# Half F tile of w3 for two chunks at once, a reordered start, and a last output in two pieces (linear attention block with MLP, one Trainium2 core)

## The chip, the cores and the metric

The kernel runs on one core of a Trainium2 chip. The metric is device microseconds of one execution; the numbers quoted are medians or means of several executions, and where two kernels are compared they were run in turn on the same chip.

TensorE (PE in the profile) is the engine everything turns on here; VectorE is DVE, ScalarE is ACT, GpSimd is POOL, and SyncE (SP) issues most of the DMA transfers.

## The reference, cut to what matters

`x` is 2048 tokens by 640, in bf16. One branch is linear attention (32 heads of 20) and ends in a product with `wo`; the other is a normalised, shifted two-layer MLP and then a second MLP through a width of 1728. A gate mixes the two.

```python
def _A_ref(x, wqkv, wo):                        # q, k, v = x @ wqkv
    phi = lambda t: jnp.where(t > 0, t + 1, jnp.exp(t)) + 1e-6
    ...
def _B_ref(x, w1, w2, w3, w4):
    ...
    x1 = x + hs                                 # hs: shifted gelu(LN(x) @ w1) @ w2
    h2 = _gelu(_layernorm(x1) @ w3) @ w4        # w3: 640 x 1728, w4: 1728 x 640
    return x1 + h2
g = sigmoid((x * gate_w).sum(-1, keepdims=True))
return g * _A_ref(x, wqkv, wo) + (1 - g) * _B_ref(x, w1, w2, w3, w4)
```

1728 is 13 tiles of 128 and a half tile of 64.

## The kernel before: the parts that matter

A scheduler in Python places work items (a group of matmuls and its evictions) in one order per engine. All matmul groups share a helper, so in the profile most of them have one line, L606. Tokens are handled in 16 tiles (`NT`) of 128 and 4 chunks (`NCH`) of 512; `KD` is 5 slices of the 640 columns; `KFF` is 13.

The start. Two loads of x rows come first, then the five slices of the query weights. While they are in flight TensorE multiplies constants ("fillers", `warmup`), so that it is busy when the work arrives. The four x tiles of the first chunk are transposed on TensorE (`t_x`, copied out by DVE for even tiles and ACT for odd ones). A small DMA ("touch") reads a few scattered pieces of the weights.

```python
    sch.dma("act", junk[:, 0, 0:32].rearrange("p (k f) -> p k f", k=2),
            A_wqkv.rearrange("(k p) f -> p k f", p=128)[:, 0:KD:KD - 1, 0:16], "touch")
    dma_in(x_tok[:, 0:2, :], x2[0:256, :]..., "x01")
    dma_in(x_tok[:, 2:4, :], x2[256:512, :]..., "x23")
    for k in range(KD):
        load_wq(k)
    # ... (key weights, gate vector)
    for c in range(1, NCH):
        dma_in(x_tok[:, 4 * c:4 * c + 4, :], x2[512 * c:512 * (c + 1), :]..., "xc%d" % c)
        for t in range(4 * c, 4 * c + 4):
            sch.dma("sp", xT[:, :, 128 * t:128 * (t + 1)], x_tok[:, t, :], ..., transpose=True)
    # ... (cut)
    NWARM = 5
    NWARM2 = 2
    # ... (cut)
    addA(("warm",), 0.0, lambda: warmup(NWARM, 427.0))
    for i in range(4):
        addA(("tx", i), 0.28, lambda i=i: t_x(i))
        if i % 2:
            addA(("warm", i), 0.0, lambda: warmup(NWARM2, 300.0))
    addA(("q", 3), 5.44, q_four)     # queries of the tiles 0 to 3, slice by slice
    addA(("k", 0), 1.36, k_first)
    for i in range(1, 4):
        addA(("k", i), 1.36, lambda t=i: k_tile(t))
```

The half tile. A matmul here has 64 weight columns and writes 64 of the 128 output partitions (`ps[64 * par:64 * par + 64]`), so two matmuls of 256 columns are placed side by side, one on each half, once per chunk. In the chain before, ten of them take 0.67 us; one after the other, at half the 0.216 us of a 512-column matmul each, they would need 1.08 us (estimate):

```python
    def w3_half(c):
        b = bank()
        jobs = []
        for k in range(KD):
            xv = xnT[:, k, 512 * c:512 * (c + 1)].rearrange("p (n h q) -> p n h q", h=2, q=128)
            for par in range(2):
                jobs.append((ps[64 * par:64 * par + 64, b, 0:256], w3[:, k, 128 * KFF:F], xv[:, :, par, :],
                             k == 0, k == KD - 1))
        # ... (ten matmuls, one per job)
        activation(h2h[:, sl, :], ps[:, b, 0:256], ACTF.Gelu_apprx_tanh)
```

The end. The last tile is evicted in two pieces (512 and 128 columns), then stored by one DMA:

```python
    def out_tiles(t0, t1):
        sch.dma("sp", out[0, 128 * t0:128 * t1, :]..., x_tok[:, t0:t1, :], ...)
```

## Time and profile before

| | before |
|---|---|
| time, median of 3 | 266.43 us (265.92 to 266.44) |
| profiled execution | 266.35 us, span 264.6 us, granted clock 1.0 |
| TensorE busy | 260.2 us, 98% |
| chain of waits | 98% TensorE |
| half tile | 4 excursions of 0.67 us |
| last eviction starts | 261.12 us |

The profile page of the kernel before. The digits are the busy share in 40 slices, in tenths; the chain is the work that ended last, followed backwards.

```profile
span 264.6 us, 4340 instructions
...
PE 260.2 (98%) x1729; PEld 136.7 (52%) x1729; DVE 145.8 (55%) x242; ACT 107.9 (41%) x218; POOL 91.4 (35%) x148
...
PE   7999999999999999999999999999999999999995
...
PEclk9999999999999999999999999999999999999999
...
PE 98%; DVE 0%; POOL 0%; issue 0%; POOLq 0%
```

TensorE is at 90% or more in every slice between the first and the last. Time can only be won by taking TensorE work away, before the first useful matmul, or after the last one. PEclk is the clock that the profile reports as granted: full speed everywhere.

The chain of waits of the kernel before; columns are start (us), duration (us), and what it was.

```profile
3.91 1.25 PE ps L617 x10
5.15 0.73 PE ps L833 x2
5.88 0.56 PE ps L617 x10
6.44 0.43 PE ps L833 x2
...
13.68 6.83 PE ps L606 x50
...
134.52 0.67 PE ps L1024 x10
...
169.85 0.67 PE ps L1024 x10
...
205.18 0.67 PE ps L1024 x10
...
240.51 0.67 PE ps L1024 x10
...
261.12 1.08 DVE x_tok L645 x2
```

The first lines are the start: ten transposes (L617), two fillers (L833), ten transposes, two fillers, after five fillers that are not shown; the queries follow. "L606 x50" at 13.68 is the first stage of dense keys; I use its first line as the moment when the start is over. L1024 are the four half tiles. The eviction of the last tile is the final line. From 13.68 to 261.12 us are 247.44 us. What follows the start of that eviction is 266.35 - 261.12 = 5.23 us of the time.

The timeline of TensorE in the kernel before: start, time until the group ends, what.

```profile
3.91 1.25 PE L617 MATMUL ps<-ident,x_tok 128*128 128x128 bf16 x10
...
5.72 0.72 PE L617 MATMUL ps<-ident,x_tok 128*128 128x128 bf16 x10
...
6.71 0.38 PE L855 MATMUL ps<-wq,xT 128*128 128x512 bf16 x1
6.92 0.22 PE L856 MATMUL ps<-wq,xT 128*128 128x128 bf16 x1
6.98 0.38 PE L855 MATMUL ps<-wq,xT 128*128 128x512 bf16 x1
```

The queries start at 6.71 us, and the next instructions follow 0.21 and 0.06 us later (such a time from one matmul's start to the next is its pitch), 0.216 and 0.056 us over the stage.

The DMA issues in the last stretch of the kernel before: size of one and microseconds from issue to landing.

```profile
out_dram<-x_tok SPq DMA_DIRECT2D x2, 160.0 KB, 1.8
```

The last of these two stores is what the end of the execution waits for: 1.8 us, of which its data move for 0.55 us (263.0 to 263.55).

### The profile page before, as it was taken

How to read it: one execution, taken by the hardware profiler on the slowest of the kernel's cores; microseconds unless marked ns; L12 is line 12 of the kernel's file. 1: busy time of each engine (PE TensorE's matmuls, PEld its weight loads, DVE VectorE, ACT ScalarE, POOL GpSimd, SP SyncE). 2: the span in 40 equal slices, each digit the busy share in tenths (PEclk: the TensorE clock that was granted, in tenths of full speed). 3: DMA queues.
4: the chain of work that ended last, by engine and by line, in shares of the span. 5: the costliest groups of instructions: out<-in, count | busy, mean ns of one | idle time of the engine just before them, and what ended most of it. 6: DMA issues, size and time to landing. Idle time of an engine off the chain costs nothing.

```text
span 264.6 us, 4340 instructions
## 1 busy us (share of the span) xinstructions
PE 260.2 (98%) x1729; PEld 136.7 (52%) x1729; DVE 145.8 (55%) x242; ACT 107.9 (41%) x218; POOL 91.4 (35%) x148
## 2 busy tenths in 40 slices
PE   7999999999999999999999999999999999999995
PEld 4555555555555555554445445545454455445553
DVE  1486877899713797999776986321212121122242
ACT  3496677741365757766651211212321322121000
POOL 4003995759764025688730204000120011021020
PEclk9999999999999999999999999999999999999999
DMA  7765998634567897255456831120000200002011
GB/s 229 218 100 133 199 182 136 191 85 22 102 122 106 252 379 137 39 99 49 92 113 126 111 63 25 42 85 2 0 0 11 90 0 0 2 0 102 0 50 50
DMA packets 50627, 24.78 MB, mean 94 GB/s; under 512 B 42028, under 2 KB 49197, under 8 KB 50608
## 3 DMA queue, kind: packets, MB, share of 16 engines
q1 hardware_dynamic: 49184, 21.23, 37.0%
q0 software_dynamic: 1152, 3.28, 5.4%
q8 instruction: 13, 0.21, 0.4%
q14 instruction: 6, 0.05, 0.1%
q10 hardware_dynamic: 272, 0.01, 0.1%
HBM read 12.05 MB, written 2.62 MB: 55 GB/s over the span
## 4 chain that ended last, share of the span: by engine, by line
PE 98%; DVE 0%; POOL 0%; issue 0%; POOLq 0%
PE ps L606 61%; PE ps L1102 21%; PE ps L785 8%; PE ps L855 2%; PE ps L833 1%; PE ps L1084 1%; PE ps L1024 1%; PE ps L617 1%; PE ps L941 1%; PE ps L856 1%; DVE x_tok L645 0%; POOL ones_c L665 0%; POOLq L1228 0%
## 5 line engine op out<-in xcount | busy, mean ns | idle before, releaser
L662 ACT ACTIVATE h2T<-ps 128x512 bf16<-128x512 f32 x52 | 31.0, 596 | 83.8 <-PE ps L606 83.7
L606 PE MATMUL ps<-xnT,w_58 128*128 128x512 bf16 x260 | 60.9, 379 | 0.0
L1102 PE MATMUL ps<-w_84,h2T 128*128 128x512 bf16 (+1 forms) x416 | 58.8, 299 | 0.0
L628 POOL TENSOR_SCALAR abx<-x_tok,stg 128x640 f32<-128x640 bf16 x16 | 13.9, 873 | 107.6 <-DVE x_tok L645 71.2
L1102 PEld LDWEIGHTS ps<-w_84,h2T 128*128 128x128 bf16 x416 | 32.7, 98 | 27.8 <-issue 1.3
L645 DVE SCALAR_TENSOR_TENSOR x_tok<-ps,stg,abx 128x640 bf16<-128x640 f32 (+2 forms) x17 | 14.3, 845 | 51.7 <-PE ps L1102 51.7
L606 PEld LDWEIGHTS ps<-xnT,w_58 128*128 128x128 bf16 x260 | 24.0, 98 | 24.8 <-issue 1.0
L645 DVE SCALAR_TENSOR_TENSOR abx<-ps,stg,abx 128x640 f32<-128x640 f32 x16 | 14.1, 882 | 27.9 <-PE ps L606 24.9
L662 ACT ACTIVATE Er<-ps 128x640 bf16<-128x640 f32 x32 | 22.4, 704 | 13.7 <-PE ps L606 8.8
L662 ACT ACTIVATE hsT<-ps 128x512 bf16<-128x512 f32 (+1 forms) x32 | 18.9, 593 | 14.6 <-PE ps L606 14.3
L661 ACT ACTIVATE junk<-x_tok 128x640 bf16<-128x640 bf16 x32 | 23.6, 736 | 2.0 <-DVE x_tok L643 1.7
L606 PE MATMUL ps<-M_sb,pqnT 128*128 128x512 bf16 (+1 forms) x160 | 24.0, 299 | 0.0
L606 PE MATMUL ps<-xnT,w_59 128*128 128x512 bf16 x100 | 23.9, 379 | 0.0
L785 PE MATMUL ps<-pk_tok,x_tok 128*128 128x512 bf16 (+1 forms) x160 | 23.9, 299 | 0.0
L606 PE MATMUL ps<-w_60,hsT 128*128 128x512 bf16 (+1 forms) x160 | 23.7, 299 | 0.0
L606 PE MATMUL ps<-wkg,xT 128*128 128x512 bf16 (+1 forms) x150 | 22.6, 300 | 0.0
L628 POOL TENSOR_SCALAR xn<-x_tok,st_54 128x640 bf16<-128x640 bf16 x16 | 17.3, 1087 | 7.1 <-DMA xnT<-xn 7.0
L606 PEld LDWEIGHTS ps<-w_60,hsT 128*128 128x128 bf16 x160 | 13.2, 98 | 12.2
L606 PEld LDWEIGHTS ps<-M_sb,pqnT 128*128 128x128 bf16 x160 | 13.1, 98 | 12.2 <-issue 0.6
L628 POOL TENSOR_SCALAR xn<-x_tok,st_55 128x640 bf16<-128x640 bf16 x16 | 16.7, 1052 | 5.1 <-DMA xnT<-xn 4.7
L606 PE MATMUL ps<-wq,xT 128*128 128x512 bf16 (+1 forms) x120 | 18.3, 299 | 0.0
L628 DVE TENSOR_SCALAR Er<-Er 128x640 bf16<-128x640 bf16 x32 | 12.0, 376 | 10.2 <-ACT Er L662 10.0
(74 smaller groups left out, 264.5 us busy)
## 6 DMA issues: line engine op xcount, KB each, us to landing
w_58<-in_B_w_dram SPq DMA_DIRECT2D x1, 2160.0 KB, 8.6
w_84<-in_B_w_dram SPq DMA_DIRECT2D x1, 2080.0 KB, 14.2
x_tok<-in_A_x_dram SPq DMA_DIRECT2D x3, 640.0 KB, 5.9
out_dram<-x_tok SPq DMA_DIRECT2D x3, 640.0 KB, 3.5
wq<-in_A_wqkv_dram SPq DMA_DIRECT2D x5, 160.0 KB, 3.8
wkg<-in_A_wqkv_dram SPq DMA_DIRECT2D x5, 160.0 KB, 3.7
wv<-in_A_wqkv_dram POOLq DMA_DIRECT2D x1, 800.0 KB, 6.0
wo_aug<-in_A_wo_dram POOLq DMA_DIRECT2D x5, 150.0 KB, 4.9
```

Source lines behind the costliest of these rows:

```text
L606: ins = e.matmul(out_ap, l, r, start=(i == 0), stop=(i == n - 1))
L617: ins = e.transpose(o, s_, ident[:])
L628: return engf(lambda e: e.tensor_scalar(out_ap, in_ap, s1, s2, op0, op1), rd, [out_ap], cost=cost)
L645: return dve(lambda e: e.scalar_tensor_tensor(out_ap, in0, scalar, in1, op0, op1), rd, [out_ap], cost=cost)
L661: return act(lambda e: e.activation(out_ap, in_ap, func, bias=bias, scale=scale, accum_out=accum), rd, wr, cost=cost)
L662: return act(lambda e: e.activation(out_ap, in_ap, func, bias=bias, scale=scale), rd, wr, cost=cost)
L785: ins = e.matmul(o, l, r, start=(t0 + q_ == 0), stop=(t0 + q_ == NT - 1))
L833: ins = e.matmul(ps[:, b, :], ones_c[:, 0:128], ones_c[:, 128:640], start=True, stop=True)
L855: e.matmul(ps[:, b, 0:512], l, w[:, k, 0:512], start=(k == 0), stop=(k == KD - 1))
L856: return e.matmul(ps[:, b + 1, 0:n2], l, w[:, k, 512:512 + n2], start=(k == 0), stop=(k == KD - 1))
L941: ins = e.matmul(o, l, r_, start=st_, stop=sp_, skip_group_check=True)
L1102: ins = e.matmul(o, l, r, start=False, stop=(i == KFF - 1))
```

## The change

Three independent parts, each meant to save TensorE time or exposed time at an end:

1. `w3_half` works on two chunks (512 columns) at a time: two excursions instead of four, with the same matmul columns in all. The halves of chunk 1 must be ready earlier, so dependencies move.
2. The first slice of the query weights is loaded between the two x pairs; the queries of the tiles 0 and 1 with that slice take the place of the last two fillers. The touch reads 80 pieces instead of 256.
3. The last output is stored in two pieces, the first while the second eviction runs.

```diff
-    h2h = rb.alloc("h2h", [128, 2, 256], BF16)
+    h2h = rb.alloc("h2h", [128, NCH, 256], BF16)
...
-    sch.dma("act", junk[:, 0, 0:32].rearrange("p (k f) -> p k f", k=2),
-            A_wqkv.rearrange("(k p) f -> p k f", p=128)[:, 0:KD:KD - 1, 0:16], "touch")
+    sch.dma("act", junk[0:16, 0, 0:80].rearrange("p (k f) -> p k f", k=KD),
+            A_wqkv[:, 0:16].rearrange("(k e r) f -> e r k f", k=KD, r=8)[:, 0, :, :], "touch")
     dma_in(x_tok[:, 0:2, :], ...)
+    load_wq(0)
     dma_in(x_tok[:, 2:4, :], ...)
-    for k in range(KD):
+    for k in range(1, KD):
         load_wq(k)
...
-    def stream(tiles, w, n2, land, done):          # order made by an assumed landing time
+    def stream(order, w, n2, done):                # order given; (t, None) transposes tile t
...
     def q_four():
-        stream(range(4), wq, 128, 0.5, lambda t, b: phi(b, pq_tok[:, t, :]))
+        order = [(0, 0), (1, 0), (2, None), (3, None), (0, 1), (1, 1), (2, 0), (0, 2), (1, 2), (3, 0), (0, 3), ...]
+        stream(order, wq, 128, lambda t, b: phi(b, pq_tok[:, t, :]))
...
-    for i in range(4):
+    for i in range(2):
         addA(("tx", i), 0.28, lambda i=i: t_x(i))
-        if i % 2:
-            addA(("warm", i), 0.0, lambda: warmup(NWARM2, 300.0))
+    addA(("warm", 1), 0.0, lambda: warmup(NWARM2, 300.0))
...
-            xv = xnT[:, k, 512 * c:512 * (c + 1)].rearrange("p (n h q) -> p n h q", h=2, q=128)
+            xv = xnT[:, k, 512 * c:512 * (c + 2)].rearrange("p (n h q) -> p n h q", h=2, q=128)
...
-                jobs.append((ps[64 * par:64 * par + 64, b, 0:256], ...))
+                jobs.append((ps[64 * par:64 * par + 64, b, :], ...))
...
+        dst = out[0, 128 * t0:128 * t1, :].rearrange("(n p) d -> p n d", p=128)
+        for n0, n1 in ((0, 512), (512, D)) if t0 == NT - 1 else ((0, D),):
+            sch.dma("sp", dst[:, :, n0:n1], x_tok[:, t0:t1, n0:n1], ...)
...
-        IT.add("W3", ("w3h", c), 0.76, lambda c=c: w3_half(c))
+        if c % 2 == 0:
+            IT.add("W3", ("w3h", c), 1.27, lambda c=c: w3_half(c), [(("t2", u), 0.9) for u in range(4 * c + 4, 4 * c + 8)])
...
-        deps4 = [(("a", t), 0.0), (("w3h", c), GEL)]
+        deps4 = [(("a", t), 0.0), (("w3h", c - c % 2), GEL), (("w3", c, KFF - 1), GEL)]
```

More of the change, by code (lines that the diff above doesn't have):

```diff
@@ L842, in q_tile @@
         phi(b, pq_tok[:, t, :])
-    def stream(tiles, w, n2, land, done):
-        nxt = {t: 0 for t in tiles}
-        bs = {t: pair() for t in tiles}
-        now = 0.0
-        while nxt:
-            t = next((t for t in tiles if t in nxt and nxt[t] * land <= now), min(nxt, key=lambda t: nxt[t]))
-            now = max(now, nxt[t] * land) + 0.272
-            k, b = nxt[t], bs[t]
+    def stream(order, w, n2, done):
+        bs = {}
+        for t, k in order:
+            if k is None:
+                t_x(t)
+                continue
+            if k == 0:
+                bs[t] = pair()
+                bank_hold.update((bs[t], bs[t] + 1))
+            b = bs[t]
             l = xT[:, k, 128 * t:128 * (t + 1)]
@@ L857, in stream @@
             pe(fn, [w[:, k, 0:512 + n2], l], [ps[:, b, 0:512], ps[:, b + 1, 0:n2]], cost=272.0)
-            nxt[t] += 1
-            if nxt[t] == KD:
-                del nxt[t]
+            if k == KD - 1:
+                bank_hold.difference_update((b, b + 1))
                 done(t, b)
     def q_four():
-        stream(range(4), wq, 128, 0.5, lambda t, b: phi(b, pq_tok[:, t, :]))
+        order = [(0, 0), (1, 0), (2, None), (3, None), (0, 1), (1, 1), (2, 0), (0, 2), (1, 2), (3, 0), (0, 3), (1, 3), (0, 4),
+                 (2, 1), (1, 4), (2, 2), (2, 3), (2, 4), (3, 1), (3, 2), (3, 3), (3, 4)]
+        stream(order, wq, 128, lambda t, b: phi(b, pq_tok[:, t, :]))
     def k_out(t, b):
@@ L870, in k_first @@
     def k_first():
-        stream(range(1), wkg, 131, 0.0, k_out)
+        stream([(0, k) for k in range(KD)], wkg, 131, k_out)
     def addA(name, dur, fn, deps=()):
@@ L1011, in w3_half @@
     def w3_half(c):
-        sl = c % 2
         b = bank()
@@ L1015, in w3_half @@
         for k in range(KD):
-            xv = xnT[:, k, 512 * c:512 * (c + 1)].rearrange("p (n h q) -> p n h q", h=2, q=128)
+            xv = xnT[:, k, 512 * c:512 * (c + 2)].rearrange("p (n h q) -> p n h q", h=2, q=128)
             for par in range(2):
-                jobs.append((ps[64 * par:64 * par + 64, b, 0:256], w3[:, k, 128 * KFF:F], xv[:, :, par, :],
-                             k == 0, k == KD - 1))
+                jobs.append((ps[64 * par:64 * par + 64, b, :], w3[:, k, 128 * KFF:F], xv[:, :, par, :], k == 0, k == KD - 1))
         def fn(e):
@@ L1025, in fn @@
             return ins
-        pe(fn, [w3[:, :, 128 * KFF:F], xnT[:, :, 512 * c:512 * (c + 1)]], [ps[:, b, 0:256]], cost=KD * 112.0 + 200.0)
-        activation(h2h[:, sl, :], ps[:, b, 0:256], ACTF.Gelu_apprx_tanh)
+        pe(fn, [w3[:, :, 128 * KFF:F], xnT[:, :, 512 * c:512 * (c + 2)]], [ps[:, b, :]], cost=KD * 218.0 + 200.0)
+        activation(h2h[:, c:c + 2, :].rearrange("p c n -> p (c n)"), ps[:, b, :], ACTF.Gelu_apprx_tanh)
     qn_slot = {}
@@ L1078, in w4_half @@
                 rows = slice(64 * par, 64 * par + 64)
-                jobs.append((ps[:, bs[2 * par + i], 0:n1 - n0], h2h[rows, sl, 128 * pr:128 * (pr + 1)], w4[rows, KFF, n0:n1]))
+                jobs.append((ps[:, bs[2 * par + i], 0:n1 - n0], h2h[rows, t // 4, 128 * pr:128 * (pr + 1)], w4[rows, KFF, n0:n1]))
         def fn(e):
@@ L1085, in fn @@
             return ins
-        pe(fn, [h2h[:, sl, 128 * pr:128 * (pr + 1)], w4[:, KFF, :]], [j[0] for j in jobs], cost=490.0)
+        pe(fn, [h2h[:, t // 4, 128 * pr:128 * (pr + 1)], w4[:, KFF, :]], [j[0] for j in jobs], cost=490.0)
     def w4_tile(t):
@@ L1115, in out_tiles @@
     def out_tiles(t0, t1):
-        sch.dma("sp", out[0, 128 * t0:128 * t1, :].rearrange("(n p) d -> p n d", p=128), x_tok[:, t0:t1, :], "out%d" % slot("out", 4))
+        dst = out[0, 128 * t0:128 * t1, :].rearrange("(n p) d -> p n d", p=128)
+        for n0, n1 in ((0, 512), (512, D)) if t0 == NT - 1 else ((0, D),):
+            sch.dma("sp", dst[:, :, n0:n1], x_tok[:, t0:t1, n0:n1], "out%d" % slot("out", 4))
     def w3_load():
```

## The prediction

> **What bounds it.** TensorE. The page gives PE 98% of a 264.6 us span at full clock; the chain of waits is 98% PE. So a gain must remove TensorE time, or lie before the first useful matmul (about 6.7 us) or after the last (about 261.9 us).
>
> **Part 1, half F tile of w3.** Four excursions of ten 128x256 matmuls (64 weight columns, two side by side) become two of ten 128x512. In the chain an excursion takes 0.67 us and the 15 matmuls behind it 2.54 us. A full 512-column matmul has a pitch near 0.216 us (1.08 us for five), a 128-column one near 0.056 us, so those 15 should take 2.44 us: 0.10 us to leave the mode. Five side-by-side pairs of 256 columns need 0.54 us (estimate, half of 1.08), so entering costs 0.13 us. Together about 0.23 us per excursion, two of which go: -0.47 us, all on the critical path. [...] the 0.23 us here is this case's price. The order of instructions moves: attention output tile 1 now precedes the first w4 tile. Its transposed input was issued at 136.4 us and takes 2.7 us; the tile would start near 140.3 us, so about 1 us is spare.
>
> **Part 2, start.** In the timeline before: five filler matmuls from 1.59 us, ten transposes 3.91, two fillers 4.95, ten transposes 5.72, two fillers 6.28, dense queries from 6.71 us. The last two fillers (0.43 us) go: queries of tiles 0 and 1 with slice 0 fill the place, and transposes of tiles 2 and 3 follow. The slice is needed at 5.7 us; issued second (near 1.3 us) with 3 to 3.8 us to landing, it is there by about 4.5 to 5.1. x rows 2-3 slip to about 5.3 us, needed at 6.3. ScalarE's copy of tile 1 ends at 5.89 us, just in time. Gain -0.43 us; the stream behind is dense, so it carries through. The lighter touch (80 small pieces, not 256) may bring the first x rows slightly earlier: 0 to -0.15 us. The gate vector lands near 11.4 us and is needed at 11.7: tight.
>
> **Part 3, end.** The last eviction ends at 262.20 us; the store is issued then, its data move 263.0 to 263.55 us, landing 1.8 us after issue. In two pieces, 512 columns go out from 261.85 us during the second eviction, and only 128 columns remain. The first's issue slot (0.37 us) delays the second by about 0.05 us. [...] Most of the 1.8 us is fixed. -0.1 us (0 to -0.25).
>
> **Sum.** -0.47 - 0.43 - 0.05 - 0.1 = about -1.05 us, from 266.43: **265.4 us**, range 264.9 to 265.95. Faster by over 2%: 0.01; within 2%: 0.98; slower: 0.01.
>
> **What would show it.** Right: two w3-half groups of about 1.2 us in the chain; x20 instead of x40; the dense query stage starting at 5.7 us and key tile 0 at 11.7 us; PE still at 98% with no new waits; last store data ending near 263.3 us minus the shift.
>
> **What would make it wrong.** A PE wait for wq slice 0, x rows 2-3 or an xT copy at 5.7 to 8 us; the gate vector late; the moved attention and w4 tiles waiting for VectorE to free PSUM banks near 150 us, where VectorE runs 3 us chains between evictions; the narrow store taking as long as the wide one.

The sum came to -0.47 - 0.43 - 0.05 - 0.1 = -1.05 us, from 266.43 to 265.4 us. The -0.05 us for the lighter touch and the -0.1 us for the end were guesses. That most of the 1.8 us is fixed rests on the 0.55 us in which the data move.

Only executions in the fast state are compared.

## The result and the profile after

| | before | after |
|---|---|---|
| time, median of 6 fast runs in turn | 266.64 us (265.92 to 266.87) | 266.3 us (266.11 to 266.51) |
| profiled execution | 266.35 us, span 264.6 | 266.33 us, span 264.6 |
| TensorE busy | 260.2 us, 98% | 258.2 us, 98% |
| dense key stage starts | 13.68 us | 14.36 us |
| last eviction starts | 261.12 us | 261.32 us |

The ratio is 0.999, with a 95% interval from 0.9976 to 1.0004. Ratios here are the mean time of one kernel's fast runs over the mean of the other's fast runs of the same rounds, so not quite the ratio of the quoted medians. Executions in which one die ran at a lower clock are left out of the means. The prediction, 265.4 us with a range of 264.9 to 265.95, is missed: 266.3 lies above it. The means differ by 0.27 us, with an interval that includes no gain at all, where 1.05 us had been announced.

The page after:

```profile
span 264.6 us, 4264 instructions
...
PE 258.2 (98%) x1675; PEld 136.4 (52%) x1707; DVE 145.9 (55%) x242; ACT 107.6 (41%) x216; POOL 91.1 (34%) x148
...
PE 96%; DMA 1%; issue 1%; ACT 0%; DVE 0%
```

The matmul count falls by 54, the count of weight loads (PEld) by 22. The 22 are real: 20 half-tile matmuls (20 left of 40) and two fillers. The other 32 are matmul records missing from this trace, so the busy time is not compared closely, and that is also where the bits of "issue" in this chain come from that lower its TensorE share to 96%; another 1% is a DMA, which comes next.

The chain of waits after:

```profile
0.80 3.27 DMA x_tok<-in_A_x_dram
...
4.12 1.25 PE ps L617 x10
...
14.36 3.17 PE ps L606 x22
...
135.20 1.20 PE ps L1025 x10
...
205.62 1.20 PE ps L1025 x10
...
261.32 1.08 DVE x_tok L645 x2
```

Two half-tile groups of 1.20 us replace four of 0.67. From 14.36 to 261.32 us are 246.96 us, against 247.44 before: the middle became 0.48 us shorter. After the start of the last eviction, 266.33 - 261.32 = 5.01 us follow, against 5.23: 0.22 less. And the start became 0.68 us longer, 14.36 against 13.68. Those three make up -0.02 us, which is the whole difference of the two profiled executions. **The gain was made and is in the trace; in this pair the first 14 us took it back.** The chain also begins with a new line: TensorE now waits for the first x rows.

The timeline of TensorE after:

```profile
4.12 1.25 PE L617 MATMUL ps<-ident,x_tok 128*128 128x128 bf16 x10 [0.21 <-DMA x_tok<-in_A_x_dram]
...
6.01 0.63 PE L858 MATMUL ps<-wq,xT 128*128 128x512 bf16 x1
6.44 0.31 PE L859 MATMUL ps<-wq,xT 128*128 128x128 bf16 x1
6.54 0.63 PE L858 MATMUL ps<-wq,xT 128*128 128x512 bf16 x1
...
7.08 1.02 PE L617 MATMUL ps<-ident,x_tok 128*128 128x128 bf16 x10
7.93 0.38 PE L858 MATMUL ps<-wq,xT 128*128 128x512 bf16 x1
8.15 0.22 PE L859 MATMUL ps<-wq,xT 128*128 128x128 bf16 x1
```

The plan worked as a sequence: queries at 6.01 us, before the second ten transposes. But the pace is wrong. The first 512-column matmul has 0.43 us to its successor (6.01 to 6.44), where in the kernel before it had 0.21. The ten transposes at 7.08 take 1.02 us, against 0.72. Only from 7.93 on does a 512-column matmul again take 0.22 us. TensorE ran at half its pace until about 7.7 us.

The granted clock for two stretches of that same profile (time, busy us and count, clock, DMA share, GB/s):

```profile
core 0: us, PE busy (x), PEclk, DMA share, GB/s
1.50:4.30 2.80, 2.50 (x7) 1.00 0.66 220
4.30:7.70 3.40, 3.40 (x22) 1.00 0.99 336
```

The clock column says 1.00 in both, though the matmuls in them came at half pace (0.427 us from one of 512 columns to the next). In this stretch the matmul pitch, not that column, tells the pace. The expectations below call the moment at which the pitch falls the release of the clock. That a clock changes there is not shown, since the column reads 1.00 before the moment and after it.

The DMA issues at the end, after:

```profile
out_dram<-x_tok SPq DMA_DIRECT2D x1, 128.0 KB, 1.7
out_dram<-x_tok SPq DMA_DIRECT2D x1, 32.0 KB, 1.5
```

The store that the end waits for now carries 32 KB and lands in 1.5 us rather than 1.8, with rows of 256 bytes.

### The profile page after: what moved, and what is told of

Its sections match the earlier page's. It is cut to its first block, busy times and chain, and to the rows that moved or that the text cites. A ratio compares the mean times of both kernels' runs of the same rounds, so it can differ in the third digit from the quotient of the medians.

```text
span 264.6 us, 4264 instructions
## 1 busy us (share of the span) xinstructions
PE 258.2 (98%) x1675; PEld 136.4 (52%) x1707; DVE 145.9 (55%) x242; ACT 107.6 (41%) x216; POOL 91.1 (34%) x148
## 4 chain that ended last, share of the span: by engine, by line
PE 96%; DMA 1%; issue 1%; ACT 0%; DVE 0%
PE ps L606 60%; PE ps L1103 21%; PE ps L786 8%; PE ps L858 2%; DMA x_tok<-in_A_x_dram 1%; PE ps L1085 1%; PE ps L1025 1%; PE ps L617 1%; PE ps L859 1%; PE ps L944 1%; DVE x_tok L645 0%; PE ps L834 0%; ACT h2T L662 0%; ACT M_sb L662 0%
## 5 line engine op out<-in xcount | busy, mean ns | idle before, releaser
L606 PE MATMUL ps<-xnT,w_58 128*128 128x512 bf16 x250 | 59.0, 379 | 0.5
L1103 PE MATMUL ps<-w_84,h2T 128*128 128x128 bf16 (+1 forms) x412 | 58.2, 298 | 0.4 <-issue 0.3
L606 PE MATMUL ps<-M_sb,pqnT 128*128 128x128 bf16 (+1 forms) x157 | 23.7, 298 | 0.2
L606 PE MATMUL ps<-w_60,hsT 128*128 128x128 bf16 (+1 forms) x158 | 23.6, 298 | 0.1
L786 PE MATMUL ps<-pk_tok,x_tok 128*128 128x128 bf16 (+1 forms) x156 | 23.3, 297 | 0.2
L606 PE MATMUL ps<-xnT,w_59 128*128 128x512 bf16 x96 | 23.2, 379 | 0.3 <-issue 0.2
L606 PE MATMUL ps<-wkg,xT 128*128 128x131 bf16 (+1 forms) x148 | 22.4, 298 | 0.1
L606 PEld LDWEIGHTS ps<-M_sb,pqnT 128*128 128x128 bf16 x160 | 13.3, 98 | 12.4 <-issue 0.4
L606 PEld LDWEIGHTS ps<-w_60,hsT 128*128 128x128 bf16 x160 | 13.3, 98 | 12.2
L606 PE MATMUL ps<-wq,xT 128*128 128x128 bf16 (+1 forms) x118 | 18.2, 298 | 0.1
```

Source lines behind the costliest of these rows:

```text
L606: ins = e.matmul(out_ap, l, r, start=(i == 0), stop=(i == n - 1))
L786: ins = e.matmul(o, l, r, start=(t0 + q_ == 0), stop=(t0 + q_ == NT - 1))
L1103: ins = e.matmul(o, l, r, start=False, stop=(i == KFF - 1))
```

## The experiments

Two numbers help to read all of them. In the fast profiles the dense middle had the same length to 0.01 us wherever its code was the same and no new wait fell in it: 247.44 us without the halves, 246.96 with them. After the start of the last eviction came 5.22 to 5.27 us without the split store and 4.98 to 5.01 with it (one outlier: 6.17 us in the profiled execution of the light touch, the excess lying outside its span). So for each kernel I subtract the middle and the end (5.22 or 5.00) from its mean time and get the mean **start**, the moment when the dense keys begin, over all its fast runs and not just the profiled one (this takes it that the middle and end are as long in the unprofiled runs; a new wait in the middle of such a run is counted into its start). For before it is 266.45 - 247.44 - 5.22 = 13.79 us (55 runs in five jobs, each on another chip). The prediction amounts to a start of 13.2 to 13.3.

| kernel | mean us | minus before of the same job | implied start |
|---|---|---|---|
| halves alone | 266.50 | +0.01 | 14.32 |
| end alone | 266.21 | -0.27 | 13.77 |
| halves and end | 265.76 | -0.73 | 13.80 |
| halves and end, again | 265.88 | -0.43 | 13.92 |
| halves and end, one more filler | 265.70 | -0.89 | 13.74 |
| start alone | 266.52 | +0.03 | 13.86 |
| start alone, again | 266.50 | +0.06 | 13.84 |
| start alone, one more filler | 266.65 | +0.22 | 13.99 |
| the change, first job | 266.29 | -0.27 | 14.33 |
| the change, again | 265.89 | -0.70 | 13.93 |
| light touch alone | 267.19 | +0.76 | 14.53 |
| new order alone, old touch | 266.49 | +0.05 | 13.83 |
| halves, end, new order, old touch | 265.63 | -0.96 | 13.67 |
| the same again | 265.80 | -0.61 | 13.84 |
| the same, last two x chunks loaded together | 265.81 | -0.60 | 13.85 |
| before, no touch | 266.72 | +0.41 | 14.06 |
| before, one filler instead of five | 267.36 | +0.76 | 14.70 |

The first four have a start whose code is that of before, and yet lie between 13.77 and 14.32. That is the scatter of one kernel's mean over six runs, and nothing smaller than about 0.3 us is read from a single row.

### Each part alone

Theory: halves and end gain what they should, and the start gives nothing or costs. Rival: the halves' new dependencies, or the attention tile that now comes earlier, cost something in the middle.

Halves alone (the `h2h`, `w3_half`, `w4_half` and dependency lines of the change, nothing else):

```diff
-            xv = xnT[:, k, 512 * c:512 * (c + 1)]...
+            xv = xnT[:, k, 512 * c:512 * (c + 2)]...
(and the other lines of part 1)
```

> Before plus the merged w3 halves alone. Theory A (each excursion left out saves 0.23 us) and theory B (the late clock release at the start ate the gain) both say: 0.45 us faster than before. If it is the same as before within 0.1 us, the halves are where the gain was lost. Profile: two w3-half pieces of 1.20 us in the chain. The clock release (pitch of 512-column matmuls falling from 0.43 to 0.22 us) is at about 5.6 us as before if it depends on the program; anywhere between 4 and 8 us if it is chance.

Measured: 266.50 us, ratio 1.0001 (0.998 to 1.0021): nothing in the mean. Its chain shows why:

```profile
5.26 0.85 PE ps L833 x2
6.11 0.80 PE ps L617 x10
...
14.15 6.83 PE ps L606 x50
...
134.99 1.20 PE ps L1022 x10
...
205.41 1.20 PE ps L1022 x10
...
261.11 1.08 DVE x_tok L645 x2
```

From 14.15 to 261.11 us are 246.96 us: the 0.48 us are there. But the start, whose instructions are those of before, took 0.47 us longer in this execution: the ten transposes took 0.80 us at 6.11 against 0.56 at 5.88, and two fillers 0.85 against 0.73; the first transposes also began 0.10 us later (4.01 us). The same code starts at 13.68 in one execution and 14.15 in another. This was the first sight of a chance in the start that the prediction hadn't reckoned with.

Start alone (the touch, the load order, `stream`, `q_four` and the first items):

```diff
+    load_wq(0)
     dma_in(x_tok[:, 2:4, :], ...)
(and the other lines of part 2)
```

> Before plus the new start with the new touch alone. Theory B, the new start delays the release of the clock: 0.3 to 0.7 us slower than before, first k tile by x5 groups from about 14.3 us instead of 13.7, release near 7.7 us as in after. Rival, the late release in the one profile of after was chance: 0.2 to 0.5 us faster than before on average.

Measured: 266.52 us over five fast runs, ratio 1.0 (0.998 to 1.002). One run was slow (275.22 us), and the profile fell on it. Part 2 on its own gains nothing that shows.

End alone (`out_tiles` only):

```diff
+        for n0, n1 in ((0, 512), (512, D)) if t0 == NT - 1 else ((0, D),):
```

> Before plus the last output in two pieces alone. Expected from the pair of profiles (3.48 us from the start of the last eviction to the end of the span before, 3.28 after): 0.1 to 0.2 us faster. Rival, that the fixed completion latency is all: 0.0.

Measured: 266.21 us, -0.27, ratio 0.9989 (0.997 to 1.0008). The mean is not decisive. In the profile the eviction starts at 260.93 us and the execution takes 265.92: 4.99 us, against 5.23. The 0.24 us is well outside the 0.05 us by which that stretch varies. The 32 KB piece landed 1.5 us after issue, against 1.8 for the 160 KB of the tile before, so the latency is mostly, but not wholly, the same for both sizes.

Halves and end:

```diff
(the lines of parts 1 and 3)
```

> After with the start undone (halves and tail only). Theory B: 0.6 us faster than before, 0.3 us faster than after. Rival (chance): 0.6 us faster than before, but 0.2 to 0.4 slower than after on average.

Measured: 265.76 us, -0.73, ratio 0.9972 (0.9948 to 0.9996). The sum of the two readings is -0.48 - 0.23 = -0.71. In this profile too the middle took 246.96 us. The rival, a cost in the middle, falls.

### The start, taken apart

Light touch alone, on before:

```diff
-    sch.dma("act", junk[:, 0, 0:32]..., A_wqkv...[:, 0:KD:KD - 1, 0:16], "touch")
+    sch.dma("act", junk[0:16, 0, 0:80]..., A_wqkv[:, 0:16]...[:, 0, :, :], "touch")
```

> Before with the lighter touch alone (80 pieces on 16 partitions for 256 on 128). So far the first x rows landed at 3.9 to 4.0 us after the span's start in four profiles with the old start and at 4.12 and 4.17 us in two with the new one. Theory T (the touch does it): landing at 4.1 to 4.2 us here, and the time 0.1 to 0.3 us longer than before. Theory O (the order of the loads does it): 3.9 us as before, time the same as before or up to 0.1 us shorter.

Measured: 267.19 us, +0.76, ratio 1.0028 (1.0006 to 1.005). The first transposes started at 4.18 us after a wait of 0.29 us for x, against 3.91 before. Lighter was not earlier. A part of the +0.76 is the scatter described above, and 0.16 us of it is the one run (268.13 us, the profiled one) whose excess lies outside its span.

The new order alone, with the old touch:

```diff
(part 2 without the two touch lines)
```

> The new order of loads and of the first queries with the old touch. Theory T: first x rows at 3.9 us, dense stage up to 0.4 us earlier than before at the same clock release, mean time 0.2 to 0.4 us shorter than before. Theory O: first x rows at 4.1 to 4.2 us, mean time within 0.2 us of before.

Measured: 266.49 us, +0.05, ratio 1.0 (0.998 to 1.002). The profile caught an execution with an early full pace:

```profile
5.41 0.38 PE L858 MATMUL ps<-wq,xT 128*128 128x512 bf16 x1
5.63 0.22 PE L859 MATMUL ps<-wq,xT 128*128 128x128 bf16 x1
5.81 0.39 PE L858 MATMUL ps<-wq,xT 128*128 128x512 bf16 x1
```

The queries begin at 5.41 us and their pitch is 0.22 us at once. Here the start is what the prediction had drawn, and dense keys begin at 12.92 us in the timeline (13.52 before). But 0.13 us passes between 5.63 + 0.06 and 5.81: the query of tile 1 waits for ScalarE's copy of its transposed x. And the gain was lost again at 42 us, where the chain runs through a DMA:

```profile
28.86 8.21 DMA x_tok<-in_A_x_dram
...
37.09 5.31 DMA xT<-x_tok
...
42.44 2.90 PE ps L606 x20
```

The third x chunk was issued at 28.86 us and landed 8.2 us later; the transposes behind it in the queue came late, and the dense keys waited for tile 12 (0.7 us in the view of waits; the stretch from the dense keys to the last eviction is 0.92 us longer than in before). An early TensorE alone doesn't make this wait: in before the same chunk landed in 6.0 us and its transposes began at 35.07 us, 2 us earlier than here.

Start alone again, and with a sixth filler to close the gap ahead of the x rows:

```diff
-    NWARM = 5
+    NWARM = 6          # second kernel only
```

> The whole new start once more (its first profile fell into the slow state). If the release of the clock is chance in both kernels, the mean is 0.2 to 0.4 us shorter than before (0.43 us of fillers less, half to all of 0.2 us of later x rows back). If the new start delays the release, the mean is the same or up to 0.5 us longer and the release lies after 6.5 us.

Measured: 266.50 us, +0.06, ratio 1.0002 (0.9982 to 1.0022). The result of the first try stands, this time with a fast profile: full pace from 5.60 us, first transposes at 4.15 us, after a wait of 0.25 us for x.

> The whole new start with six fillers ahead of the first transposes instead of five, so that the gap of 0.2 to 0.4 us in which PE waits for the first x rows is closed. If a gap in PE's activity delays the release of the clock: mean 0.3 us or more shorter than the new start with five, release at 5.0 to 6.5 us. If the release is a matter of chance alone: within 0.15 us of it.

Measured: 266.65 us, +0.22, ratio 1.0008 (0.9989 to 1.0026). Filling the gap gained nothing that shows. In its profile the first transposes still began at 4.17 us, and the full pace came at 6.14.

### When the full pace comes

From the starts of successive matmuls in each trace I read the moment at which the pitch of a 512-column matmul falls from 0.427 to 0.216 us, called the release below. (Before: 5.63 us; after: 7.71.) At a pitch of 0.427 us the matmuls take twice as long as at 0.216, so a release one microsecond later costs about half a microsecond (estimate from the two pitches, the half rule below). The release, and the start of the dense keys in the timeline:

| profile | first transposes | release | dense keys | dense keys minus half the release |
|---|---|---|---|---|
| old start: before | 3.91 | 5.63 | 13.52 | 10.71 |
| end alone | 3.86 | 5.32 | 13.33 | 10.67 |
| halves and end | 3.89 | 5.15 | 13.27 | 10.70 |
| halves alone | 4.01 | 6.53 | 13.99 | 10.73 |
| halves and end, again | 3.89 | 7.05 | 14.19 | 10.67 |
| old order, light touch | 4.18 | 7.09 | 14.36 | 10.82 |
| new order and light touch: after | 4.12 | 7.71 | 14.20 | 10.35 |
| after, again | 4.15 | 7.09 | 13.91 | 10.37 |
| start alone, again | 4.15 | 5.60 | 13.30 | 10.50 |
| start alone, one more filler | 4.17 | 6.14 | 13.47 | 10.40 |
| new order, old touch | 4.05 | 4.60 | 12.92 | 10.62 |
| halves, end, new order, old touch | 3.86 | 4.92 | 12.97 | 10.51 |
| the same again | 4.01 | 4.72 | 13.07 | 10.71 |
| the same, last two x chunks loaded together | 4.05 | 6.60 | 13.64 | 10.34 |

In the first five rows only the release differs, and the last column stays within 0.06 us while the keys move by 0.9. So the release accounts for the spread of the old start. (Left out are the profiles with another number of fillers on the old start, with no touch, or with earlier x chunks.)

For one and the same release, the rows with the new order lie 0 to 0.36 us below the 10.70 of the old start. The three with the earliest release (4.60 to 4.92 us) gain least, 0 to 0.19: there TensorE waits for ScalarE's copy of the transposed x (0.13, 0.26 and 0.18 us), and in "the same again" 0.1 us more for the x rows of tile 2, which landed at 6.19 us where the prediction had about 5.3. The four with a release after 6 us gain 0.30 to 0.36. A part of what is missing to the predicted 0.43 goes with the light touch: against the one profile with it and the old order (10.82), the four rows with the new order and the light touch lie 0.32 to 0.47 us lower. So beside the same touch and with a late release the order's price comes out about right; that rests on a single profile.

Is the release driven by what TensorE does? One filler instead of five, on before:

```diff
-    NWARM = 5
+    NWARM = 1
```

> Before with one filler matmul instead of five ahead of the first transposes, so PE works from 1.6 to 2.0 us and then idles until 3.9 us. [...] Then the earliest release moves about 1.7 us later and the mean time grows by 0.7 to 1.0 us[...]. If the release does not depend on PE's activity, time and range stay as before (within 0.2 us).

The 1.7 us is the author's estimate, the four fillers left out at 0.427 us each.

Measured: 267.36 us, +0.76, ratio 1.0027 (1.0007 to 1.0047).

```profile
3.85 1.25 PE L617 MATMUL ps<-ident,x_tok 128*128 128x128 bf16 x10 [1.66 <-POOL hsT L665]
...
5.75 1.12 PE L617 MATMUL ps<-ident,x_tok 128*128 128x128 bf16 x10
```

TensorE stands idle for 1.66 us ahead of the transposes, both groups of transposes run at half pace (1.25 and 1.12 us), and the release came at 6.58 us. The direction is that of a release driven by activity, but that is not shown: 6.58 us also lies within what the old start shows by chance (5.15 to 7.05), and the light touch alone, with all five fillers, had the same +0.76.

The change once more, in a later job:

```diff
(the change, unaltered)
```

> The changed kernel once more. If halves (-0.48 us) and output (-0.23 us) are sure and the start is worth -0.1 to 0.1 us on average, with the moment of the clock release drawn by chance, the mean is 0.6 to 0.8 us below before. If the new start really costs 0.4 us, as its first six runs suggest, 0.2 to 0.4 us below before.

Measured: 265.89 us, -0.70, ratio 0.9972 (0.9952 to 0.9993). The first job's -0.27 and this -0.70 are the same kernel. Over both jobs, -0.27 and -0.70 average to about -0.5 us.

Halves, end and new order, with the old touch:

```diff
(the change without the two touch lines)
```

> The changed kernel with the old touch. If the lighter touch is what delays the first x rows, they land at 3.9 to 4.05 us, and the mean is 0.1 to 0.3 us below the changed kernel's and at or slightly below that of halves and output alone (0.73 us below before in its run).

Measured: 265.63 us, -0.96, ratio 0.9959 (0.994 to 0.9977), the best of all. Its profile has an early release (4.92 us) and again the wait near 42 us (1.0 us).

Halves and end with earlier fillers, on a tile that VectorE fills with ones:

```diff
+    memset(dve, xn[:, 0, :], 1.0)
-    NWARM = 5
+    NWARM = 6
-                ins = e.matmul(ps[:, b, :], ones_c[:, 0:128], ones_c[:, 128:640], start=True, stop=True)
+                ins = e.matmul(ps[:, b, :], xn[:, 0, 0:128], xn[:, 0, 128:640], start=True, stop=True)
```

> Halves and output on the old start, with the filler operand set by VectorE in its own tile, so that the fillers start near 1.1 to 1.2 us instead of 1.59, and six of them. [...] the earliest release moves 0.3 to 0.4 us earlier, the mean gets 0.15 to 0.25 us shorter than halves and output alone, 0.85 to 1.0 us below before. Rival (release independent of activity): 0.7 us below before, as without it.

The 0.3 to 0.4 us were the author's estimate for fillers that start 0.4 to 0.5 us earlier.

Measured: 265.70 us, -0.89, ratio 0.9965 (0.9944 to 0.9987). The premise failed: VectorE's memset ran from 1.00 to 1.59 us, so the fillers began at 1.65 us, no earlier than the 1.59 before. The kernel is then halves and end with one more filler, and the row tells nothing about early fillers. Its profile has the earliest release of all, 4.37 us.

Before without any touch:

```diff
-    sch.dma("act", junk[:, 0, 0:32]..., "touch")
```

> Before without any touch. If the lighter touch is worse because it touches less [...], the first x rows land as late as with it or later (4.1 us or more) and the mean is 0.3 us or more above before. If the light touch is itself the hindrance, the first x rows land at 3.9 us or earlier.

Measured: 266.72 us, +0.41, ratio 1.0019 (1.0004 to 1.0034). The first transposes began at 3.80 us, the earliest of all, and yet the profile's release came at 7.71. In this profile early x rows brought no early release with them. What a touch does to later reads, no run here shows.

Halves and end again:

```diff
(the lines of parts 1 and 3)
```

> Halves and output on the old start once more, beside the two above: 0.6 to 0.8 us below before; the sum of -0.48 and -0.23 us read from the profiles is -0.71.

Measured: 265.88 us, -0.43, ratio 0.9988 (0.9971 to 1.0004). With the -0.73 of its first job, the average is -0.58; the reading from the chain is -0.71.

### Is the wait at 42 us where an early start is lost?

Two profiles had shown it: both with dense keys before 13.0 us and the last transposes issued from 37 us. The first try loads all x chunks before any of their transposes:

```diff
     for c in range(1, NCH):
         dma_in(x_tok[:, 4 * c:4 * c + 4, :], ..., "xc%d" % c)
+    for c in range(1, NCH):
         for t in range(4 * c, 4 * c + 4):
             sch.dma("sp", xT[...], x_tok[:, t, :], ..., transpose=True)
```

> Halves, output and new order with the old touch, and the three later x chunks issued one after the other instead of each behind the transposes of the chunk ahead. Theory (the transposed x of tile 12 is a floor at 42.4 to 42.7 us that takes back what the start gained when the third chunk is slow): no wait of PE for transposed x anywhere, last four transposes issued before 33 us, mean 0.1 to 0.4 us below the same kernel without it (0.96 below before in its run), so 1.0 to 1.3 us below before. If the floor matters in few executions: within 0.1 us of that kernel.

Measured: 266.98 us, +0.67, ratio 1.0029 (1.0008 to 1.005): worse.

> Halves and output on the old start with the early x chunks. On the old start the group of tile 12 begins at 42.1 to 42.8 us, so the floor hardly bites: within 0.15 us of halves and output alone (0.73 us below before). If it gains as much as the new order does, the floor was not tied to the start.

Measured (the same edit on halves and end, with the old start): 267.07 us, +0.76, ratio 1.0032 (1.0018 to 1.0047). Both made a new wait: the first chunk's transposes came later, and the keys waited 1.8 and 0.7 us for tile 4. In the first of them the gate vector also landed at 12.23 us (10.9 to 11.6 in the profiles without this edit), and the keys of tile 0 began at 12.32 us, 0.4 us after the queries were through: the prediction had called this vector tight. The edit moved the wait instead of taking it away, so it couldn't answer the question.

The second try leaves the first chunk alone and loads the other two together behind its transposes; beside it the same kernel without the edit:

```diff
-        dma_in(x_tok[:, 4 * c:4 * c + 4, :], ..., "xc%d" % c)
+        for c_ in ((1,), (2, 3), ())[c - 1]:
+            dma_in(x_tok[:, 4 * c_:4 * c_ + 4, :], ..., "xc%d" % c_)
```

> Kernel: the change with the old touch (as g3), and the third and fourth x chunk loaded together, right after the first chunk's transposes, so that no later transposes sit between them in the queue. Floor theory (what an early start gains is lost again at a wait for the transposed x of tile 12 near 42 us when the third chunk lands slowly): no wait of TensorE for a transposed x above 0.1 us in the key stage, the last four transposes issued before 33 us, and a mean 0.1 to 0.4 us below the same kernel without this edit (next run), 0.9 to 1.3 us below before. Rival (the floor is rare, or the early start is not common): the mean within 0.15 us of the next run. Third: the load of two chunks at once delays tile 8's transposes and makes a new wait near 33 us; then the mean is 0.3 us or more above the next run.

> Kernel: the same as g3 (the change with the old touch), run again beside the one before it. If the halves (-0.48 us) and the end (-0.23 us) hold and the new order with the old touch gains 0.1 to 0.25 us, the mean lies 0.7 to 1.0 us below before. If the -0.96 us of g3 was chance: 0.4 to 0.7 us below. Release of the clock (pitch of the 512-column matmuls falling to half) anywhere from 4.4 to 7.7 us; if the profile shows tile 0's dense keys starting before 13.0 us and the last four transposes issued after 36 us, a wait of 0.5 to 1.0 us near 42 us; otherwise none.

Measured: 265.81 us with the edit and 265.80 without it; -0.60 and -0.61 against before, ratios 0.9978 (0.9956 to 0.9999) and 0.9977 (0.9955 to 0.9998). The queue of SP with the edit, then without:

```profile
23.83 10.58 SPq L279 DMA_TRANSPOSE xT<-x_tok  x8
```

```profile
36.24 5.67 SPq L279 DMA_TRANSPOSE xT<-x_tok  x4
```

With the edit, eight transposes follow each other from 23.83 to 34.41 us, the last four from about 29 us; the last of all started near 33.1, just past the 33 us of the expectation. No wait for a transposed x is left. Without it, the last four begin at 36.24 us, and this execution (keys at 13.07 us) had no wait either. The means are equal, which is what the rival says, but each of the two ratios is known only to about 0.2%, 0.5 us, so a gain of 0.1 to 0.4 us is not excluded; and the profile with the edit had a late release (6.60 us), so its start was not an early one. The wait at 42 us is real where it was seen, in two of the three profiles of the new order with the old touch and the old loads. How much of the mean it holds back stays open. The implied start with no such wait seen is still 13.85 us.

## Why the prediction was wrong, point by point

**Halves: right.** "Together about 0.23 us per excursion, two of which go: -0.47 us, all on the critical path." The chain gives -0.48 us from the first dense key to the last eviction, the same 246.96 us in after, halves alone and halves and end. The 0.23 us was worked out beforehand from two differences in the old chain (0.67 - 0.54 us to enter, 2.54 - 2.44 us to leave; the 0.54 and 2.44 are estimates from the pitches), so it's a price that a profile shows before anything is changed.

**Order of the attention tile, VectorE, gate vector: no harm**, as predicted or hoped; the middle of the chain has no new wait of size, and the gate vector landed at 10.93 us in the profile after, well before the keys of tile 0 (12.82).

**End: right mechanism, too small.** Predicted -0.1 (0 to -0.25), measured about -0.23 us. The 32 KB piece, with rows of 256 bytes, landed in 1.5 us and the 128 KB piece in 1.7, against 1.8 for the undivided 160 KB; a narrow store as slow as the wide one, a risk that the prediction had listed, did not come.

**Start: the step that failed.** The text says "Gain -0.43 us; the stream behind is dense, so it carries through" and that the lighter touch "may bring the first x rows slightly earlier: 0 to -0.15 us". In sum that made the start 0.48 us shorter. The marks it set, queries at 5.7 us and the keys of tile 0 at 11.7, came out at 6.01 and 12.82 us in the profile after (12.14 before, for the keys). Measured, as implied means: 13.83 us for all kernels with the old order and touch (85 runs), 13.99 for those with the new order and the light touch (29 runs), and 13.78 for the new order with the old touch (18 runs). So the new order gave about -0.05 us and the light touch about +0.2; together +0.16 us rather than -0.48. With a scatter of about 0.25 us between kernels of one and the same start, "no gain, perhaps a loss of up to 0.3" is the safe reading. Three things stand in the place of the step:

- *The moment of release was taken as fixed.* The profile before was a single execution with a release at 5.63 us; others of the same start code had 5.15 to 7.05. In the pair of profiles the release came 2.08 us later (7.71 against 5.63), which by the half rule costs 1.04 us; the new order and touch gave 0.36 us back (10.71 - 10.35); together that is the 0.68 us by which the start grew. So in the pair the saving was made, and the release took it back. The pitch at 512 columns was 0.427 us ahead of the release and 0.216 behind it in both profiles, and over all fast profiles the release spreads over 4.4 to 7.7 us, 3.3 us. What sets the moment is not shown by any run here; that TensorE's activity decides was theory.
- *An early TensorE meets what it needs too soon.* "The stream behind is dense, so it carries through" did not hold with an early release: the queries of the first slice waited 0.13 to 0.26 us for ScalarE's copy of the transposed x, and in two of three such profiles the dense keys waited again near 42 us (0.7 and 1.0 us), a loss that the implied start of 13.78 us includes. The prediction named the first as a risk ("ScalarE's copy of tile 1 ends at 5.89 us, just in time") and then booked the gain in full.
- *The lighter touch was followed by later x rows.* The first transposes began at 4.12 to 4.18 us in five profiles with it, and at 3.85 to 4.05 us in those with the old one (leaving out the one whose six fillers ran until 4.18). That sign is shown; its reason isn't.

**The range.** A spread of the release of 3 us is worth 1.5 us from one execution to the next (estimate by the half rule). The 55 runs of before have a standard deviation of 0.45 us, so the mean of six still moves by about 0.2 us (estimate, 0.45 over the root of six). The range of +-0.5 us knew nothing of this. The first job's after (start 14.33) was on the late side, the second (13.93) nearer the middle; the second's median, 265.96, misses the range by a hundredth.

The sum as it came out: -0.48 (halves) - 0.23 (end) + 0.16 (start) = -0.55 us, against about -0.5 measured over both jobs. This is no independent test, since the start is what the means leave over and 12 of its 29 runs are the change's own.

**Left open.** Why the x rows land later behind a lighter touch; whether the new order makes the release later on average (at equal release its kernels with the light touch start about 0.3 us earlier, in the mean 0.16 us later, which would need a release some 0.9 us later, an estimate by the half rule; but each kernel has one profile or two, and the release of unprofiled runs isn't recorded); and how often the wait at 42 us occurs. A better version: the change with the old touch had the lowest mean of all and a middling one (-0.96 and -0.61 us, 12 runs), below before by an interval that excludes 1 both times. Against the change itself (-0.27 and -0.70), or halves and end alone (-0.73 and -0.43), the advantage of 0.2 to 0.3 us is no larger than the scatter.

## What to carry to other kernels

A profile is one execution: before pricing something in the first ten microseconds, look at the matmul pitch to see when TensorE's pace doubled there (here from 0.427 to 0.216 us at 512 columns, at 4.4 to 7.7 us), and profile the unchanged kernel several times to see whether that moment moves. Work taken out of a dense stretch (half-tile excursions in the middle) was worth here what the old chain had said, to a hundredth (0.48 us against 0.47); a store that could start earlier gave 0.22 us in the pair and 0.24 alone. Work taken out of the first microseconds, where operands are just arriving, was worth less (0 to 0.36 us of 0.43 at an equal moment of doubling), since with an early doubling the engine came sooner to an operand that wasn't there (waits of 0.13 to 0.26 us), and the moment itself moved by more than the work was worth. When a total hides under chance, cut the trace at marks where the code is identical on both sides and compare the parts.
